# Pairing head h with head h+4 in an attention and expert kernel: fewer, larger transfers of q and k, and a new written order

## The chip, the core and the metric

The kernel runs on one core of one Trainium2 chip. The metric is device time in microseconds (us) of one execution of the whole program. The kernel before took 605.56 us as the median of three runs (602.78 to 605.9).

The core has five engines that run side by side and each in its own order: TensorE (PE, matrix products), VectorE (DVE), ScalarE (ACT), GpSimd (POOL) and SyncE (SP), which here only issues transfers. Transfers are carried out by 16 DMA engines. PE writes to PSUM, a small memory of banks, and the other tiles lie in SBUF, which has 128 partitions.

## The reference

The inputs q, k, v are 8 batches x 8 heads x 576 positions x 64 values in float32. Two attentions are added: one over means of four neighbouring positions (144 of them), repeated four times, and one in which a position sees only those less than four away. The result, as 4608 rows of 512 values (8 heads side by side), goes through a feed-forward part with 1024 hidden values.

```python
q_d, k_d, v_d = (t.reshape(B, H, 144, 4, D).mean(axis=3) for t in (q, k, v))
out_up = np.repeat(sm_attn(q_d, k_d, v_d), 4, axis=2)
mask = np.abs(pos[:, None] - pos[None, :]) < 4
out_local = softmax(where(mask, q @ k.T / 8, -1e9)) @ v
x = (out_up + out_local).transpose(0, 2, 1, 3).reshape(4608, 512)
h = x @ w_in
solu = h * softmax(h)
out = (solu - mean) / sqrt(var + 1e-6) * g_ln @ w_out
```

w_in and w_out come in as float64, 8 bytes a value.

## The kernel before

**Tiles.** The eight heads of a batch are held as four pairs. A tile such as `qT` has 128 partitions, 64 of them for each head of a pair, and four pairs along its rows. Pair r holds heads 2r and 2r+1. The rows of a 128-row block of w_in then belong to one pair, because the feed-forward part multiplies a tile `xh` of 128 tokens pair by pair with `wi_h[:, cc]`.

**Loading q and k.** For batches 0 and 1 (`EarlyBatch`), `load_one` (L477 to L483) brings one pair of q or of k in one transfer of 288 KB, and PE transposes it (L496). For batches 2 to 7 `load_q_k` (L244) brings them in a layout that VectorE can transpose in blocks of 32 x 32: 128 partitions are four quadrants of 32, one for each head of the pair and each half of its 64 values. One call brings one pair with 8 transfers of 72 KB (four quadrants, q and k), so a batch has 32 transfers, each of 32 x 18 pieces of 128 bytes. `pair_steps` then transposes k (L423), sums it by fours (`kd`), transposes q (L427) and sums it. There is one buffer for q and one for k.

**Values.** `load_vw` (L256) brings windows of 64 positions for the local attention, `load_vs` and `load_tail` (L277, L284) bring v for the sums by fours. `Local` and `PairOfLocals` compute the local attention of one and of two groups of windows, `Pooled` the other.

**Weights.** `Weights` (L300) has 16 pieces of 512 KB: eight of w_in (block cc of 128 rows, half n of the columns) and eight of w_out. `load(n)` brings one with one transfer (L325); `piece(n)` makes float32 of it and splits it into a high and a low part, with seven steps on ScalarE, VectorE and GpSimd (L334 to L374). The pieces of w_in with numbers 0, 1, 6 and 7 pass through the tile `stage`, the others through tiles named `w`.

**The feed-forward part.** 36 tiles of 128 tokens. `ffn_in` has 24 matmuls into `h` (L779), which need all eight pieces of w_in, then the softmax steps; the tile `e` is stored to `u` in DRAM (L827) and read back rearranged as `v` (L859), transposed on VectorE (L880), split into `uh` and `ul` (L886, L889), and multiplied with w_out in 24 matmuls into `o` (L903). `osb` is the scaled result (L910), stored at L912.

**Order.** The Python loops at the end only make a list of steps, `plan`, batch by batch. The work is emitted in the order of the numbers in `ORDER`, an order over all steps written out by hand or by a search; every engine executes its instructions in that order, and SP its transfers. `OTHER` is the list of steps that use the other of two engines for a step that either can do (`engine(usual, instead)`): for instance `ul` goes to VectorE and not to GpSimd. `keep_clock` steps are matmuls on a tile of zeros, 24 in all, placed in the first 110 us.

Of the kernel before, what the change touches and what calls it, by code (L numbers as in the profile page):

```python
# [124 lines left out]
def pooled_local_attention_then_solu_ffn(  # L125
# [10 lines left out]
    nc = tc.nc  # L136
    P = 128
    B, H, S, D = q.shape
    FAC = 4
# [245 lines left out]
    class Batch:  # L385
# [27 lines left out]
        def load_q_k(self, pr):  # L413
            load_q_k(self.qk, self.b, pr)
# [650 lines left out]
```

## Time and profile before

| what | value |
|---|---|
| median of three runs | 605.56 us |
| the profiled execution's own time | 605.33 us |
| its span, first to last instruction | 603.5 us |
| mean granted TensorE clock | 0.963 of full speed |
| busy: PE, VectorE, ScalarE, GpSimd | 93, 76, 51, 51% of the span |
| moved by DMA | 99.70 MB in 208,271 packets, mean 165 GB/s |

The page of the profile has the busy time of each engine, the span in 40 slices with tenths of busy time, and the chain of work that ended last. A line such as "L249" is a line of the kernel. "SPq" is the queue of SyncE: time in which a transfer was being issued. "PEld" is the loading of weights into TensorE, which overlaps with its products. "PEclk" and "granted clock" are the share of full clock that TensorE was given. The DMA share is the mean busy share of the 16 DMA engines. A packet is one contiguous piece that one DMA engine moves.

### The profile page before, as it was taken

To read this page: it belongs to the slowest core of one execution; us is meant where nothing else is said; L and a number is where in the kernel's file an instruction comes from. 1 tells how busy PE (TensorE), PEld (TensorE's weight loads), DVE (VectorE), ACT (ScalarE), POOL (GpSimd) and SP (SyncE) were. 2 spreads that over 40 slices of the span, in tenths; PEclk is the share of its full clock that TensorE was granted. 3 is DMA by queue.
4 is the path that set the end of the run, shared out by engine and by line. 5 is a ranking of instruction groups with operands and counts; after the bars stand their busy time and mean duration, and the time that the engine had idled before them with its cause. 6 is when DMAs were issued, how large, how long until landed. Compare 5 with 4: busy or idle time off the path is not lost.

```text
span 603.5 us, 16899 instructions
## 1 busy us (share of the span) xinstructions
PE 560.4 (93%) x6728; PEld 436.9 (72%) x6728; DVE 459.0 (76%) x716; ACT 306.1 (51%) x639; POOL 308.1 (51%) x457
## 2 busy tenths in 40 slices
PE   7877978799899999979989999998999999999996
PEld 4655656577677777757767777776877777787885
DVE  3999987999787888768877876777888867654641
ACT  2466763576544564544534654454534547342443
POOL 5476574657385374554635564544637523532111
PEclk9698998799899999989998999998999999999999
DMA  8998658876878677797587877667672642333230
GB/s 237 243 233 147 136 123 171 210 185 136 189 182 161 194 205 206 136 250 185 153 216 155 207 206 168 160 164 183 182 196 77 200 136 81 107 122 123 88 123 35
DMA packets 208271, 99.70 MB, mean 165 GB/s; under 512 B 164288, under 2 KB 194496, under 8 KB 208192
## 3 DMA queue, kind: packets, MB, share of 16 engines
q1 hardware_dynamic: 208192, 98.62, 65.1%
q8 instruction: 53, 0.87, 0.6%
q14 instruction: 26, 0.21, 0.1%
HBM read 65.54 MB, written 27.79 MB: 155 GB/s over the span
## 4 chain that ended last, share of the span: by engine, by line
PE 42%; DVE 16%; SPq 16%; DMA 12%; issue 6%; POOL 5%; ACT 2%; DVEq 0%; POOLq 0%; ACTq 0%
PE h L779 18%; PE o L903 18%; SPq L249 6%; SPq L666 4%; DMA w<-in_moe_w_out_dram 2%; DMA stage<-in_moe_w_in_dram 2%; SPq L859 2%; PE po L755 2%; DMA v<-u 2%; SPq L268 2%; DMA qm<-in_q_dram 1%; DVE nmx L787 1%; DMA u<-e 1%; DVE kd L381 1%; PE sd L717 1%
## 5 line engine op out<-in xcount | busy, mean ns | idle before, releaser
L903 PE MATMUL o<-wo_h,uh 128*128 128x512 f32 x288 | 118.1, 410 | 5.4 <-ACT osb L910 5.4
L779 PE MATMUL h<-wi_h,xh 128*128 128x512 f32 x288 | 119.7, 416 | 1.4 <-DVE e L794 1.4
L779 PE MATMUL h<-wi_l,xh 128*128 128x512 f32 x288 | 116.6, 405 | 0.0
L779 PE MATMUL h<-wi_h,xl 128*128 128x512 f32 x288 | 116.3, 404 | 0.0
L903 PE MATMUL o<-wo_l,uh 128*128 128x512 f32 x288 | 115.0, 399 | 0.0
L889 POOL TENSOR_TENSOR ul<-v,uh 128x512 fp32r<-128x512 f32 x46 | 60.8, 1325 | 53.2 <-ACT uh L886 41.9
L903 PE MATMUL o<-wo_h,ul 128*128 128x512 f32 x288 | 79.5, 398 | 0.0
L791 ACT ACTIVATE e<-h,nmx 128x1024 f32<-128x1024 f32 x36 | 40.1, 1115 | 68.4 <-DVE nmx L787 64.2
L903 PEld LDWEIGHTS o<-wo_h,uh 128*128 128x128 f32 x288 | 54.7, 190 | 21.0 <-ACT osb L910 6.2
L779 PEld LDWEIGHTS h<-wi_h,xh 128*128 128x128 f32 x288 | 56.0, 194 | 16.7 <-DVE e L794 2.0
L880 DVE STREAM_TRANSPOSE v<-v 128x512 f32<-128x512 f32 x70 | 46.5, 690 | 25.6 <-DMA v<-u 24.5
L779 PEld LDWEIGHTS h<-wi_h,xl 128*128 128x128 f32 x288 | 55.9, 194 | 14.0 <-DVE xl L937 0.3
L779 PEld LDWEIGHTS h<-wi_l,xh 128*128 128x128 f32 x288 | 56.0, 194 | 12.4
L903 PEld LDWEIGHTS o<-wo_h,ul 128*128 128x128 f32 x288 | 54.7, 190 | 13.3
L886 ACT ACTIVATE uh<-v 128x512 fp32r<-128x512 f32 x70 | 42.9, 623 | 41.0 <-DVE v L880 21.9
L903 PEld LDWEIGHTS o<-wo_l,uh 128*128 128x128 f32 x288 | 54.8, 190 | 11.9
L787 DVE TENSOR_REDUCE nmx<-h 128x1 f32<-128x1024 f32 x36 | 43.6, 1211 | 24.5 <-PE h L779 24.5
L794 DVE SCALAR_TENSOR_TENSOR e<-h,e 128x1024 f32<-128x1024 f32 x36 | 43.6, 1212 | 14.4 <-ACT e L791 14.4
L799 POOL TENSOR_SCALAR nmu<-su 128x1 f32<-128x1 f32 x36 | 8.5, 237 | 76.9 <-DVE e L794 75.7
L836 ACT ACTIVATE e<-e 128x1024 f32<-128x1024 f32 x35 | 36.8, 1052 | 20.5 <-DMA u<-e 20.5
L817 ACT ACTIVATE e<-e,nmu 128x1024 f32<-128x1024 f32 x24 | 27.6, 1148 | 32.2 <-POOL nmu L799 32.2
L910 ACT ACTIVATE osb<-o,s 128x512 f32<-128x512 f32 x36 | 24.5, 679 | 32.3 <-PE o L903 13.5
(122 smaller groups left out, 1042.7 us busy)
## 6 DMA issues: line engine op xcount, KB each, us to landing
u<-e SPq DMA_DIRECT2D x35, 512.0 KB, 3.3
v<-u SPq DMA_DIRECT2D x140, 128.0 KB, 3.4
out_dram<-osb SPq DMA_DIRECT2D x36, 256.0 KB, 2.9
vs<-in_v_dram SPq DMA_DIRECT2D x64, 128.0 KB, 3.6
qm<-in_q_dram SPq DMA_DIRECT2D x96, 72.0 KB, 2.9
km<-in_k_dram SPq DMA_DIRECT2D x96, 72.0 KB, 2.5
vw<-in_v_dram SPq DMA_DIRECT2D x80, 64.0 KB, 2.9
vw<-in_v_dram SPq DMA_DIRECT2D x40, 128.0 KB, 3.3
```

The lines of the kernel that those rows point to most:

```text
L249: nc.sync.dma_start(t[nm][Q * 32:Q * 32 + 32, pr], src[b, 2 * pr + par, :, dh * 32:dh * 32 + 32].rearrange("(k t) d -> t k d", t=32),)
L779: nc.tensor.matmul(hps[:, n, :], src[:, cc, :], wt[:, cc, n * 512:(n + 1) * 512], start=(cc == 0 and src is xh and wt is wi_h), stop=(cc = ...
L787: nc.vector.tensor_reduce(out=nmx, in_=hf, op=ALU.max, axis=AX.X, negate=True)
L791: nc.scalar.activation(e, hf, AF.Exp, bias=nmx, scale=1.0, accum_out=se)
L794: nc.vector.scalar_tensor_tensor(out=e, in0=hf, scalar=1.0, in1=e, op0=ALU.mult, op1=ALU.mult, accum_out=su)
L817: nc.scalar.activation(e, e, AF.Identity, bias=nmu, scale=1.0)
L836: nc.scalar.activation(e0, e, AF.Square, accum_out=m2)
L880: nc.vector.transpose(vg, vg)
L886: nc.scalar.activation(uh, tp, AF.Copy)
L889: (usual if v is None else engine(usual, nc.vector)).tensor_tensor(out=ul, in0=tp, in1=uh.bitcast(F32), op=ALU.subtract)
L903: nc.tensor.matmul(o, src[:, j, :], wt[:, 4 * g + j, :], start=(g == 0 and j == 0 and src is uh and wt is wo_h), stop=(g == 1 and j == 3 a ...
L910: nc.scalar.activation(osb, o, AF.Copy, scale=s)
```

## The change

Pair r now holds heads r and r+4. The four heads of one parity of all pairs (heads 0 to 3, or 4 to 7) are then neighbours in DRAM, and one transfer with one stride brings one quadrant of q, or of k, for all four pairs: 288 KB, 32 x 72 pieces of 128 bytes. `load_q_k` is called eight times a batch with one transfer each (first the four quadrants of k in the list, then those of q), and not four times with eight each; the list of steps is 24 longer (1871). The transposes and sums of the four pairs stay as they were.

The other places that name heads follow: v's windows, v for the sums, the tail and the early batches' q and k are read with the new head numbers, in as many transfers of the same sizes as before. The blocks of w_in now take the 64 rows of head r and the 64 rows of head r+4, in one transfer as before.

`ORDER` is a new order of all steps; it was found by a search in which transfers came late at random. `OTHER` is new too, 77 steps and not 78: among others `ul` is on VectorE 21 times and not 12, the sum of `vs` 6 times and not 3, the subtraction in `PairOfLocals` 2 times and not 5.

```diff
-    def load_q_k(t, b, pr):
-        for nm, src in (("q", q), ("k", k)):
-            for par in range(2):
-                for dh in range(2):
-                    Q = 2 * par + dh
-                    nc.sync.dma_start(
-                        t[nm][Q * 32:Q * 32 + 32, pr],
-                        src[b, 2 * pr + par, :, dh * 32:dh * 32 + 32].rearrange(
-                            "(k t) d -> t k d", t=32
-                        ),
-                    )
+    def load_q_k(t, b, nm, Q):
+        src = {"q": q, "k": k}[nm]
+        par, dh = divmod(Q, 2)
+        nc.sync.dma_start(
+            t[nm][Q * 32:Q * 32 + 32],
+            src[b, 4 * par:4 * par + 4, :, dh * 32:dh * 32 + 32].rearrange(
+                "r (k t) d -> t r k d", t=32
+            ),
+        )
...
-                    v[b, par::2, s0:s0 + W, :].rearrange("h s d -> s h d"),
+                    v[b, 4 * par:4 * par + 4, s0:s0 + W, :].rearrange("h s d -> s h d"),
...
-            src = v[b, 2 * w + par, 0:(NKB - 1) * KB * FAC].rearrange(
+            src = v[b, 4 * par + w, 0:(NKB - 1) * KB * FAC].rearrange(
...
-            src = v[b, 2 * w:2 * w + 2, (NKB - 1) * KB * FAC:].rearrange(
+            src = v[b, w::4, (NKB - 1) * KB * FAC:].rearrange(
...
+            by_pair = w_in.rearrange("(a r d) c two -> r a d c two", a=2, d=D)
             self.src = [
-                w_in[cc * P:(cc + 1) * P, n * 512:(n + 1) * 512, :]
-                for cc in range(NCC) for n in range(2)
+                by_pair[cc, :, :, n * 512:(n + 1) * 512, :] for cc in range(NCC) for n in range(2)
             ] + [w_out[fc * P:(fc + 1) * P, :, :] for fc in range(NFC)]
...
-                t, src[self.b, 2 * pr:2 * pr + 2].rearrange("h (p t) d -> p h (t d)", t=self.TT)
+                t, src[self.b, pr::4].rearrange("h (p t) d -> p h (t d)", t=self.TT)
...
-                            bt.vw[u + n][rows(wi), 2 * pr + par, :],
+                            bt.vw[u + n][rows(wi), 4 * par + pr, :],
...
-            else:
-                step(bt.load_q_k, pr)
+            elif pr == 0:
+                for nm in ("k", "q"):
+                    for Q in range(4):
+                        step(bt.load_q_k, nm, Q)
```

The numbers in `ORDER` and `OTHER` are left out here.

More of the change, by code (lines that the diff above doesn't have):

```diff
@@ L411, in room, with load_q_k @@
             }
-        def load_q_k(self, pr):
-            load_q_k(self.qk, self.b, pr)
+        def load_q_k(self, nm, Q):
+            load_q_k(self.qk, self.b, nm, Q)
         def load_v(self, u):
```

181 rows, old and new, of tables (ORDER, OTHER) are left out of this document.

## The prediction

> **What bounds the kernel now.** I read the page first: busy line, slices, chain of waits.
>
> ```profile
> span 603.5 us, 16899 instructions
> PE 560.4 (93%) x6728; PEld 436.9 (72%) x6728; DVE 459.0 (76%) x716; ACT 306.1 (51%) x639; POOL 308.1 (51%) x457
> ...
> PE   7877978799899999979989999998999999999996
> ...
> PEclk9698998799899999989998999998999999999999
> ...
> PE 42%; DVE 16%; SPq 16%; DMA 12%; issue 6%; POOL 5%; ACT 2%; DVEq 0%; POOLq 0%; ACTq 0%
> ```
>
> TensorE is the bound: 560.4 of 603.5 us. An order can only win from the 43.1 us that it idles and from slow clock after gaps. Next, the windows by stage (span; PE, PEld, DVE, ACT, POOL busy; granted clock; DMA share; GB/s).
>
> ```profile
> 0.00:45.00 45.00, 34.43 (x550) 24.95 (x551) 34.83 (x60) 20.48 (x50) 25.81 (x30) 0.89 0.94 238
> 45.00:130.00 85.00, 70.67 (x1184) 52.20 (x1180) 75.64 (x124) 50.11 (x102) 51.44 (x53) 0.90 0.74 159
> 130.00:300.00 170.00, 161.18 (x2096) 127.18 (x2095) 139.47 (x220) 91.25 (x193) 98.81 (x150) 0.98 0.76 183
> 300.00:450.00 150.00, 145.88 (x1664) 114.53 (x1662) 115.91 (x174) 74.04 (x156) 76.73 (x117) 0.97 0.73 181
> 450.00:590.00 140.00, 139.86 (x1207) 111.81 (x1207) 91.70 (x139) 65.60 (x134) 53.65 (x104) 1.00 0.37 119
> ```
>
> PE idles 10.6, 14.3, 8.8, 4.1 and 0.1 us in these stages: it is lost early. The first 45 us are the stage of the transfers (share 0.94), the next 85 that of VectorE (75.6 of 85). The first h matmul needs all eight pieces of w_in; it starts here (timeline), behind the last step of such a piece on VectorE:
>
> ```profile
> 57.62 0.69 DVE L349 SCALAR_TENSOR_TENSOR w<-stage,w 128x512 int32<-128x512 int32 x1
> ...
> 65.29 0.50 PE L779 MATMUL h<-wi_h,xh 128*128 128x512 f32 x1
> ```
>
> **The part that I expect to decide: w_in's rows.** `Weights.src` took 128 consecutive rows of w_in for piece (cc, n). It now takes two blocks of 64 rows, 256 rows apart (`a=2, d=64`). They can't be joined into one run of rows, so the source is a pattern of 2 x 64 x 4 KB where it was 128 x 4 KB. What does that do to the spread over the 16 DMA engines? Here is one 512 KB transfer by itself (transfers in the window 540.9 to 543.6) and the loads of w_in (by source line):
>
> ```profile
> DMA packets 145, 0.54 MB, mean 200 GB/s; under 512 B 16, under 2 KB 16, under 8 KB 144
> ...
> q1 hardware_dynamic: 144, 0.52, 47.7%
> ...
> u<-e SPq DMA_DIRECT2D x1, 512.0 KB, 2.6
> ```
> ```profile
> L325 SPq DMA_DIRECT2D stage<-in_moe_w_in_dram x4: 346/386/1068, 0.7 to 38.3; - x4
> L325 SPq DMA_DIRECT2D w<-in_moe_w_in_dram x4: 346/398/499, 2.6 to 19.6; - x4
> ```
>
> The lone transfer has 128 packets of 4 KB and 16 small ones, one completion for each engine. Its time is 47.7% of 2.7 us on 16 engines: 20.6 us of engine time, 0.161 us a packet. Spread over 16 engines a w_in piece costs each 1.3 us; if it is divided by its outermost count, two engines do 64 packets each, 10.3 us, and the eight pieces hold those two for 82.4 us. Every other transfer is also dealt to these two engines, in turn, and waits behind.
>
> Which end? Every transfer of this trace has an outermost count of 128, 96, 64, 32 or 16, all multiples of 16, so the rows neither confirm nor exclude a division by that count. 1.3 and 10.3 us are both open, and the nearest row (the lone transfer) gives the price of either, not the choice. As w_in's new pattern is the one that leaves this family, I take two engines, at two chances in three. The Trainium skill ("DMA: Bandwidth & Descriptors", section "Why a DMA increments its semaphore by 16 and not by 1") says that the division is by the slowest dimension other than 1, over the largest count up to 16 that divides it on both sides; by that rule it is two engines here and the sum below stands, without it the sum of the rival. No run here shows a spread below 16 yet.
>
> When does the last piece land then? In the new ORDER these stand ahead of `weights.load(7)` on SP's queue: the other seven pieces, 14 q or k loads of batches 0 and 1 (288 KB), three vw loads (four of 64 KB each), two vs (four of 128 KB) and the tail (four of 32 KB): 6.1 MB beside w_in. At the first window's rate (238 GB/s at share 0.94, so 253 when full) that is 24 us of each engine; at the lone transfer's (4096 B in 0.161 us, 407 GB/s over 16) 15 us. Landing: 0.7 + 82.4 + 15 to 24 = 98 to 107 us. Behind it come Abs and clamp, and then VectorE's 16 instructions between that piece's shift and `ffn_in(0)` in the new ORDER, about 11 us by these rows (grouped by form), among them four like the first two and three like the third:
>
> ```profile
> L345 DVE SCALAR_TENSOR_TENSOR w<-w,w 128x512 int32<-128x512 int32 x12 | 10.5, 878 | 0.2
> L349 DVE SCALAR_TENSOR_TENSOR w<-w,w 128x512 int32<-128x512 int32 x12 | 10.0, 840 | 0.1
> L551 DVE TENSOR_TENSOR pl<-sc,mask 128x512 f32<-128x512 f32 x20 | 13.4, 676 | 0.8 <-PE sc L539 0.7
> L336 DVE TENSOR_SCALAR w<-w 128x512 f32<-128x512 f32 x12 | 6.5, 538 | 4.8 <-ACT w L334 4.7
> L334 ACT ACTIVATE w<-w 128x512 f32<-128x512 f32 x12 | 8.0, 670 | 15.1 <-DMA w<-in_moe_w_out_dram 10.8 <-DMA w<-in_moe_w_in_dram 2.3 <-POOL wo_l L374 2.0
> ```
>
> Before, the way from the last such step to h was 65.3 - 56.9 = 8.4 us, so I use 8.4 to 12 (0.67 + 0.54 + 11). The first h starts between 98 + 8.4 = 106 and 107 + 12 = 119 us, which is 41 to 54 us later than 65.3; middle 48. Nothing covers it: PE executes in order, and ahead of `ffn_in(0)` stand only the matmuls of batch 0 and the first of batch 1, about as many as before. Behind it the same list of matmuls follows.
>
> **The q and k loads.** 192 transfers of 576 packets become 48 of 2304; packets and bytes stay. By source line (ns min/median/max), by timeline and by the transfers of 180 to 188.4:
>
> ```profile
> L249 SPq DMA_DIRECT2D qm<-in_q_dram x96: 311/496/1697, 49.5 to 413.5; - x96
> L249 SPq DMA_DIRECT2D km<-in_k_dram x96: 312/496/2015, 55.9 to 417.2; - x96
> ...
> DMA to landing us min/median/max: 2.0/2.6/5.5
> ```
> ```profile
> L262 SPq DMA_DIRECT2D vw<-in_v_dram x40: 595/634/2392, 197.1 to 472.8; - x40
> ```
> ```profile
> L268 SPq DMA_DIRECT2D vw<-in_v_dram x80: 595/615/1921, 30.8 to 456.1; - x80
> ```
> ```profile
> 184.06 2.12 SPq L249 DMA_DIRECT2D qm<-in_q_dram  x4
> ```
> ```profile
> 180.00:188.40 8.40, 7.26 (x106) 5.79 (x106) 6.93 (x11) 4.89 (x8) 6.55 (x9) 1.00 0.84 140
> ```
>
> An issue costs SP 0.496 us, 95 us for 192. For a transfer of four times the packets there is no row. From below: L262 has 512 packets and L268 256, and they differ by 19 ns, so 1728 more packets add 0.13 us: 0.63 x 48 = 30 us, 65 saved. From above: SP is held while the packets drain, four times 0.53 us each, 102 us, nothing saved. I take the lower price, its rows being the direct comparison. But the DMA engines are at 0.84 while four loads go out per 2.12 us, so delivery can quicken only to 0.84 of it: a batch's 32 loads from 17.0 to 14.3 us.
>
> What is SP's time worth? The chain shows one place where it ends in an idle PE:
>
> ```profile
> 254.02 1.75 SPq L249
> ...
> 256.95 3.13 DMA u<-e
> ...
> 262.46 7.41 PE o L903 x24
> ...
> 331.64 5.60 PE h L779 x24
> ```
> ```profile
> PE o L903 <- ACT osb L910: 5.4, 2, 4.1
> ```
>
> The u store waits behind 24 loads, PE waits 4.1 us for osb, and the next 24 matmuls take 7.41 instead of 5.60: 5.9 us at most. Against it: a transpose of any pair now needs all four quadrants (1.18 MB, 1.18 / (140 / 0.84) = 7.1 us from the first packet) where it needed its own four loads (2.1 us), and a quadrant can be loaded only when all four pairs of the batch before are transposed. In the new ORDER batch 3's last three k loads and batch 6's last two stand at the same place among the matmuls as the first k transposes: up to 5 us late at two places, hidden if SP has run ahead to them. I take -4 for loads and order together, from -12 (a quarter of the idle) to +12 (both waits, each with 1 us of slow clock).
>
> **OTHER, vs, tails, early loads.** ul goes from VectorE 12 times to 21:
>
> ```profile
> L889 POOL TENSOR_TENSOR ul<-v,uh 128x512 fp32r<-128x512 f32 x46 | 60.8, 1325 | 53.2 <-ACT uh L886 41.9 <-issue 4.5 <-DMA qm<-in_q_dram 3.8
> ...
> L889 DVE TENSOR_TENSOR ul<-v,uh 128x512 fp32r<-128x512 f32 x24 | 18.7, 778 | 10.2 <-ACT uh L886 10.1
> ```
>
> That is 7 us more on VectorE and 12 less on GpSimd; other moves go both ways (`pl` subtracts leave VectorE, `vs` sums come). After 450 us VectorE has 48 us to spare. Zero, inside the range above; without that cover at most 7 us. The heads' strides change in vs, tail, vw and the early loads, not their counts: zero.
>
> **Sum**, against the profiled execution's own time of 605.33 us (span 603.5, 1.8 around it; the median of the runs is 605.56): 605.3 + 48 - 4 = 649. Own range 605.3 + 41 - 12 = 634 to 605.3 + 54 + 12 = 671.
>
> **Rivals.**
> *All 16 engines serve w_in; the loads win.* No +48. SP's 16% of the chain speaks for it, PE's 0.1 us of idle after 450 against a large gain. Place: 130 to 450 us, where 12.9 us idle; price: 5.9 us at the store, and as much again of that idle as SP's 65 us reach, so about -7: 598 (592 to 602). It holds from the point that a piece lands before 45 us, as now. Faster, where I forecast slower.
> *All 16 engines, late quadrants.* Two waits of 5 us with slow clock and no gain: 605.3 + 10 = 615, with some gain 609. For it the equal places in ORDER, against it that SP issues ahead.
> *It does not do what it says.* SP is held for the packets, the engines stay at 0.84, PE's order is as full as before: 605.
>
> **How the numbers follow.** Chances: two engines 0.67, loads win 0.22, late quadrants 0.06, nothing 0.05. A measurement here tells from no change about 0.5%, 3 us. So faster 0.22, same 0.05, slower 0.73. The range from 596 to 668 holds most of the first case (0.6), the two between (0.11) and a fair part of the second (0.13). The likeliest case alone is 634 to 671.
>
> **What would show it.** Right: the w_in loads land 10 us apart or more, DMA share in the first 90 us is low (two of 16 engines: near 0.13 plus the rest's), the last `w<-stage` step is near 105 us and the first h near 112, and from there to the end the time is within 10 us of the 538 us before. Wrong: the first h before 70 us with the share again at 0.9. Of the loads: 0.63 us an issue and under 35 us in all, or about 2 us each. Late quadrants would be waits of kT for km with idle PE at sc of batches 3 and 6. The u store should go out without 24 loads ahead of it.

## The result and the profile after

The changed kernel takes 653.68 us (median of four runs, 649.22 to 655.75); the kernel before 605.53 (602.78 to 605.9). The ratio is 1.0796, with a 95% interval from 1.0725 to 1.0866. The forecast was 649.

The page of the changed kernel, in the same parts as before:

```profile
span 650.1 us, 16688 instructions
PE 559.6 (86%) x6728; PEld 435.3 (67%) x6728; DVE 461.2 (71%) x724; ACT 309.8 (48%) x645; POOL 293.7 (45%) x443
...
PE   3135434998999999799998999999999999999997
...
PEclk9996757698999999999998999999999999999999
DMA  2333344978799688668874867795745345422420
```

The work of TensorE is the same (559.6 us, before 560.4). The loss lies in the first seven slices, where PE is at 1 to 5 tenths and the DMA engines at 2 to 4, where they were at 6 to 9. Both idle at once. The line of the queue says why; it is quoted for the kernel before and then for the changed one (packets, MB, share of 16 engines):

```profile
q1 hardware_dynamic: 208192, 98.62, 65.1%
```
```profile
q1 hardware_dynamic: 205776, 98.61, 58.7%
```

2416 packets fewer. The loads of q and k are 144 transfers fewer, each with 16 completions: 2304. What is left is 112, which is 14 for each of the eight loads of w_in: each has two completions where it had sixteen. I read this as two engines for the transfer of 2 x 64 rows; the runs with sixteen, four and eight engines below test it.

The chain of waits of the changed kernel around the last piece of w_in, and the start of h in the timeline (start, length, what):

```profile
96.05 14.71 DMA stage<-in_moe_w_in_dram
...
110.84 0.66 ACT w L333
...
115.27 2.12 PE qp L495 x24
117.39 1.06 PE xp L589 x32
118.44 2.12 PE kp L495 x24
```
```profile
126.28 0.50 PE L778 MATMUL h<-wi_h,xh 128*128 128x512 f32 x1
```

The last piece is issued at 96.05 and in use at 110.84; h starts at 126.3 and not at 65.3. In between the chain runs over PE at a low clock: 24 transposes take 2.12 us (367 ns each in the median, 246 in e1_split below). Ahead of the first h PE idles 69.8 us (126.3 less 56.5 busy), and 14.1 in the kernel before. Most of it is spent at the first transposes of q, whose loads stand among the pieces of w_in on SP's queue (us in total, times, longest; the kernel before has 2.0 there):

```profile
PE qp L495 <- DMA qm<-in_q_dram: 50.5, 4, 18.6
```

The windows of the changed kernel (columns as in the prediction), the last three shifted by the 46 us:

```profile
45.00:90.00 45.00, 17.77 (x306) 11.35 (x306) 17.05 (x30) 10.02 (x33) 11.67 (x10) 0.69 0.34 101
90.00:126.00 36.00, 24.05 (x531) 20.03 (x535) 22.04 (x37) 17.12 (x30) 14.21 (x13) 0.67 0.64 160
...
176.00:346.00 170.00, 160.76 (x2095) 125.57 (x2093) 142.34 (x221) 92.16 (x205) 100.73 (x150) 0.99 0.80 187
346.00:496.00 150.00, 148.62 (x1746) 116.84 (x1744) 124.35 (x190) 77.95 (x162) 75.00 (x115) 0.99 0.67 169
496.00:636.00 140.00, 139.69 (x1214) 110.74 (x1205) 92.87 (x140) 67.62 (x138) 46.72 (x96) 1.00 0.41 129
```

From the first h to the end the changed kernel needs 650.1 - 126.3 = 523.8 us and the kernel before 603.5 - 65.3 = 538.2. So the start loses 61.0 us and the rest wins 14.4. In that rest PE is busy 503.2 us and idles 20.6, where it was busy 509.2 and idle 29.0: of the 14.4 us, 8.4 are less idle time and 6.0 are less busy time for nearly the same matmuls (5732 and 5725), at a granted clock of 0.99 and not 0.97. Two questions for the chip: is it w_in's two engines that lose the 61, and what wins the 14?

### The profile page after: what moved, and what is told of

Its sections match the earlier page's. It is cut to its first block, busy times and chain, and to the rows that moved or that the text cites. A ratio compares the mean times of both kernels' runs of the same rounds, so it can differ in the third digit from the quotient of the medians.

```text
span 650.1 us, 16688 instructions
## 1 busy us (share of the span) xinstructions
PE 559.6 (86%) x6728; PEld 435.3 (67%) x6728; DVE 461.2 (71%) x724; ACT 309.8 (48%) x645; POOL 293.7 (45%) x443
## 4 chain that ended last, share of the span: by engine, by line
PE 48%; DMA 18%; SPq 15%; DVE 10%; issue 3%; ACT 3%; POOL 2%; DVEq 0%; POOLq 0%; ACTq 0%
PE h L778 20%; PE o L902 20%; DMA w<-in_moe_w_in_dram 3%; SPq L480 3%; SPq L267 3%; DMA v<-u 3%; DMA stage<-in_moe_w_in_dram 2%; SPq L665 2%; DMA vs<-in_v_dram 2%; DMA u<-e 2%; DMA km<-in_k_dram 2%; SPq L858 2%; SPq L324 2%; PE po L754 2%; PE xp L589 1%
## 5 line engine op out<-in xcount | busy, mean ns | idle before, releaser
L778 PE MATMUL h<-wi_h,xh 128*128 128x512 f32 x288 | 118.1, 410 | 5.0 <-DVE e L793 5.0
L778 PE MATMUL h<-wi_h,xl 128*128 128x512 f32 x288 | 114.4, 397 | 0.0
L778 PE MATMUL h<-wi_l,xh 128*128 128x512 f32 x288 | 114.4, 397 | 0.0
L778 PEld LDWEIGHTS h<-wi_h,xh 128*128 128x128 f32 x288 | 54.6, 190 | 20.3 <-issue 5.9
L888 POOL TENSOR_TENSOR ul<-v,uh 128x512 fp32r<-128x512 f32 x37 | 49.1, 1332 | 37.3 <-ACT uh L885 18.7
L778 PEld LDWEIGHTS h<-wi_h,xl 128*128 128x128 f32 x288 | 54.4, 189 | 13.2
L495 PE MATMUL qp<-ident,qm 96*64 96x96 f32 x192 | 14.7, 328 | 50.7 <-DMA qm<-in_q_dram 50.5
L786 DVE TENSOR_REDUCE nmx<-h 128x1 f32<-128x1024 f32 x36 | 43.7, 1213 | 19.5 <-PE h L778 19.4
L335 DVE TENSOR_SCALAR w<-w 128x512 f32<-128x512 f32 x15 | 6.5, 440 | 62.6 <-ACT w L333 62.6
L495 PEld LDWEIGHTS qp<-ident,qm 96*64 96x64 f32 x192 | 13.0, 197 | 53.4 <-DMA qm<-in_q_dram 35.7
```

The costliest lines, as they stand in the source:

```text
L495: nc.tensor.matmul(tp[rows(par), t // HT, at:at + self.TP], self.qk[nm, pr][:, par, t], ident[0:self.TP, 0:self.TP], start=True, stop=True,)
L778: nc.tensor.matmul(hps[:, n, :], src[:, cc, :], wt[:, cc, n * 512:(n + 1) * 512], start=(cc == 0 and src is xh and wt is wi_h), stop=(cc = ...
L786: nc.vector.tensor_reduce(out=nmx, in_=hf, op=ALU.max, axis=AX.X, negate=True)
L888: (usual if v is None else engine(usual, nc.vector)).tensor_tensor(out=ul, in0=tp, in1=uh.bitcast(F32), op=ALU.subtract)
```

## The experiments

Theory: a transfer is divided over the engines by its outermost count, and this alone makes the changed kernel slow. Rival: the new order, or quadrants that come late, make the start slow.

**Two loads of 64 rows for a piece of w_in (e1_split).**

```diff
-            nc.sync.dma_start(hl, self.src[n])
+            if n < 2 * NCC:
+                for half in range(2):
+                    nc.sync.dma_start(hl[half * D:half * D + D], self.src[n][half])
+            else:
+                nc.sync.dma_start(hl, self.src[n])
```

> The changed kernel, but each piece of w_in comes in two transfers of 64 consecutive rows. Theory (each transfer is divided by its outermost count, so the one transfer of 2 x 64 rows ran on two engines): both halves run on 16 engines, 8 x 14 more completion packets than the changed kernel and 8 x 16 for the added transfers, the first h at 60 to 70 us and not 126.3. From the first h to the end the changed kernel took 523.8 us and the kernel before 538.2; if that gain belongs to the new order and loads, 65 + 524 + 1.8 = 591 us; if it was only lent by the long wait ahead of it, 598 to 605 us. Rival (the new order or the late quadrants made the start slow): the first h stays after 100 us and the time above 640 us.

Measured: 592.18 us, ratio to the kernel before 0.9824 (0.9796 to 0.9851). It is faster than both kernels. The queue has 206016 packets: 8 x 30 more than the changed kernel, 16 completions for each of 16 halves. First h and windows:

```profile
66.04 0.50 PE L782 MATMUL h<-wi_h,xh 128*128 128x512 f32 x1
```
```profile
0.00:45.00 45.00, 29.63 (x544) 21.68 (x546) 35.72 (x63) 21.40 (x51) 20.43 (x29) 0.89 0.99 217
45.00:130.00 85.00, 74.77 (x1318) 55.92 (x1314) 74.31 (x127) 54.38 (x108) 59.16 (x63) 0.90 0.84 197
130.00:300.00 170.00, 162.13 (x2055) 127.05 (x2054) 141.50 (x217) 90.33 (x195) 98.78 (x148) 0.98 0.77 184
300.00:450.00 150.00, 148.40 (x1788) 116.34 (x1786) 124.04 (x190) 77.85 (x160) 73.77 (x112) 0.99 0.66 167
```

The loss is gone with this one edit, so the rival falls. And the 14 us were hardly lent by the long wait: from the first h to the end this kernel takes 592.0 - 66.0 = 526.0 us, the changed one 523.8. The 2.2 us between them are less than the spread of the changed kernel's four runs (6.5 us), so 12 to 14 belong to order and loads together. Against the kernel before, PE is busy 4.8 us less in the first 45 us, 4.1 more between 45 and 130, 1.0 more up to 300 and 2.5 more up to 450.

**The kernel before, w_in read as 2 x 64 rows (e2_before_two).**

```diff
-                w_in[cc * P:(cc + 1) * P, n * 512:(n + 1) * 512, :]
-                for cc in range(NCC) for n in range(2)
+                by_pair[cc, :, :, n * 512:(n + 1) * 512, :] for cc in range(NCC) for n in range(2)
```

> The kernel before with one line changed: a piece of w_in is read as 2 x 64 rows in one transfer, as in the change (its rows are then those of other heads, so its result isn't the reference's; nothing is left out). Theory of two engines: completions fall by 8 x 14 = 112 packets, the last piece lands after 95 us, the first h starts at 105 to 130 us, the time is 645 to 665 us with the old order and the old 192 loads. Rival (order or loads): 603 to 608 us as before.

Measured: 659.91 us (one run), 208080 packets, which is exactly 112 fewer. The first h starts at 122.4 us, 57 us late. The old order with the old loads loses nearly as much; the pattern of w_in is enough by itself.

**Four and eight blocks (e3_four, e4_eight).**

```diff
-            by_pair = w_in.rearrange("(a r d) c two -> r a d c two", a=2, d=D)
+            by_pair = w_in.rearrange("(a r d) c two -> r a d c two", a=4, d=D // 2)   # e4: a=8, d=D // 4
```

> The changed kernel, but a piece of w_in is read as 4 x 32 rows in one transfer (4 blocks 128 rows apart; the rows then don't fit the heads, so the result isn't the reference's; nothing is left out). Theory (division by the outermost count): 4 completions a transfer, 205776 + 8 x 2 = 205792 packets on the queue; 32 packets of 0.161 us on each of four engines, 5.2 us a piece, 41 us for eight, so the last piece lands some 41 us earlier than in the changed kernel (110.8), near 70 us; the first h at 78 to 88 us and the time 604 to 614 us. Rival (any source that isn't one run of rows is slow): as the changed kernel, 650 us.

> The same with 8 x 16 rows (8 blocks 64 rows apart; result not the reference's, nothing left out). Theory of the outermost count: 8 completions a transfer, 205776 + 8 x 6 = 205824 packets, 2.6 us a piece, 21 us for eight, which hides beside the other transfers of the first 45 us: first h at 64 to 70 us, 590 to 597 us, like e1_split with 8 issues fewer. Rival: 650 us.

Measured (one run each): 619.96 us with 205792 packets, and 605.34 us with 205824. The completions are those of 4 and 8 engines to the packet, as the theory says. The Trainium skill ("DMA: Bandwidth & Descriptors", "Why a DMA increments its semaphore by 16 and not by 1") has the number of engines by the slowest count other than 1 of both sides, and one completion for each engine that takes part; the counts of 2, 4, 8 and 16 here agree with both. The times were later than expected. These are the first h, SP's issue of the last of w_in and the DMA share (from the traces) beside the time that eight pieces hold a loaded engine, 82.4 us by the lone transfer divided out:

```
engines for w_in              16     8      4      2
eight pieces hold an engine   10.3   20.6   41.2   82.4 us
last of w_in issued by SP     45.6   52.6   67.1   96.0 us
DMA share of the first 45 us  0.99   0.77   0.50   0.30
first matmul of h             66.0   75.1   94.6   126.3 us
time of the kernel            592.2  605.3  620.0  653.7 us
```

The steps of the first h (9.0, 19.5, 31.7) follow the steps of the load (10.3, 20.6, 41.2), the last one least. I had expected eight engines to hide; they don't. A reason that fits the table: in e1_split the DMA engines are at 0.99 in the first 45 us, so there is no spare time for an uneven load, and with eight, four and two engines the others stand idle while SP issues the rest later.

**What do the merged loads win? (e5_cut, e6_old_order)** e5_cut cuts each quadrant's load into four again, in the new order:

```diff
+        for pr in range(NPR):
+            nc.sync.dma_start(t[nm][Q * 32:Q * 32 + 32, pr],
+                src[b, 4 * par + pr, :, dh * 32:dh * 32 + 32].rearrange("(k t) d -> t k d", t=32))
```

> e1_split, but each quadrant's load is cut again into four transfers of one pair each, 72 KB, issued one after the other at the same place: 192 and not 48 issues, same bytes, same packets of data, same order. Theory (the DMA engines, not SP's issuing, set how fast the loads come): e1_split + 0 to 3 us, although SP is busy some 65 us longer. Rival (the fewer issues are what is gained): e1_split + 7 us or more.

Measured: 609.63 us, ratio 1.0103 (1.0071 to 1.0135), 17 us more than e1_split, measured beside it. My theory, that issuing hardly counts, falls. The first h differs by 1.3 us only. The timelines of SP's queue, e1_split and then e5_cut, show where it goes on:

```profile
63.73 0.60 SPq L248 DMA_DIRECT2D km<-in_k_dram  x1
...
88.06 0.43 SPq L328 DMA_DIRECT2D w<-in_moe_w_out_dram  x1
...
94.68 1.96 SPq L862 DMA_DIRECT2D v<-u  x4
```
```profile
63.88 2.22 SPq L249 DMA_DIRECT2D km<-in_k_dram  x4
...
91.51 0.43 SPq L329 DMA_DIRECT2D w<-in_moe_w_out_dram  x1
...
99.71 1.97 SPq L863 DMA_DIRECT2D v<-u  x4
```

Both reach the first k load at 63.8. e5_cut issues the piece of w_out 3.5 us later and the read-back of u 5.0 us later. PE waits for that piece of w_out by way of ScalarE, which has it in its order just ahead of the step plT that PE needs. ScalarE starts on the piece at 92.8 us in e1_split, after 7.8 us of idle, and at 98.2 in e5_cut, after 11.1. The row of e1_split:

```profile
92.78 0.66 ACT L337 ACTIVATE w<-w 128x512 f32<-128x512 f32 x1 [7.83 <-DMA w<-in_moe_w_out_dram]
```

PE's own wait at plt, e1_split and then e5_cut:

```profile
PE plt L583 <- ACT plT L234: 6.1, 1, 6.1
```
```profile
PE plt L584 <- ACT plT L234: 10.3, 1, 10.3
```

SP's queue is issuing nearly all the time: summed over its timeline from 60 to 300 us, 231.5 of 240 us in the kernel before, 220.4 in e1_split, 227.9 in e5_cut. (A row of several transfers counts the short gaps within it; the issues alone are 209.6, 208.0 and 213.6.) Time in which SP is held on an issue counts in this too, so a full queue doesn't show by itself that it sets the time.

e6_old_order is e1_split with the old ORDER and OTHER; a batch's eight merged transfers are issued where its first load stood:

```diff
+        def load_once(self):
+            if not self.loaded:
+                self.loaded = True
+                for nm in ("k", "q"):
+                    for Q in range(4):
+                        load_q_k(self.qk, self.b, nm, Q)
```

> e1_split with the ORDER and OTHER of the kernel before: the pairing h, h+4 and the merged transfers stay, all eight of a batch are issued at the place where the old order has the batch's first load. Theory (the order brings what there is to bring, the loads little): 600 to 608 us, near the kernel before. Rival (the merged loads bring it): as e1_split within 3 us. A third way: all eight transfers in one place hold up others behind them on SP and DMA: above 608 us.

Measured: 617.17 us, ratio 1.0228 (1.0187 to 1.0268): the third way. Its PE waits and its window from 300 to 450 us, where PE is busy 12.5 us less than in e1_split:

```profile
PE po L762 <- POOL vd L461: 10.2, 2, 8.6
PE h L786 <- DVE e L801: 9.2, 4, 4.8
```
```profile
300.00:450.00 150.00, 135.93 (x1563) 107.01 (x1562) 109.11 (x165) 70.90 (x150) 73.87 (x113) 0.94 0.67 166
```

Why vd comes late on GpSimd there wasn't followed further. So neither half wins alone: the old order with 192 loads takes 603.0 us, the new one with 192 takes 609.6, the old one with 48 in one place 617.2, the new one with 48 592.2. How the old order would do with the 48 spread out wasn't tried, since a pair's transpose stands there ahead of loads of other pairs.

**Is it SP's issuing? (e7_issues, e13_one)** Tiny extra transfers, three or one behind each merged load:

```diff
+        for _ in range(3):   # e13_one: range(1)
+            n = extra[0]
+            extra[0] += 1
+            nc.sync.dma_start(idle[0:32, 2 * n:2 * n + 2], src[b, 4 * par, 0:32, 0:2])
```

> e1_split with three tiny extra transfers (32 pieces of 8 bytes, to a place that nobody reads) behind each of the 48 loads of a quadrant: 144 issues more, as many as in e5_cut, almost no bytes. Theory (SP's issue time is what e5_cut lost: SP is busy 39 of 40 us from 60 to 100 us): 603 to 612 us, near e5_cut's 609.6. Rival (cutting costs in the DMA engines, by smaller transfers of data): 592 to 596 us.

> e7_issues with one tiny transfer behind each quadrant's load and not three: 48 issues more than e1_split (592.2 us), where 144 more gave 650.4. Theory (SP's queue is full from 60 to 300 us, 92% there in e1_split, so each added issue at these places costs its time): a third of the 58 us, 605 to 615 us. Rival (there is room for the first ones, and it is only beyond some number that they cost): 592 to 600 us.

Measured: 650.36 us (ratio 1.0794, 1.0747 to 1.084) and 608.48 us (ratio 1.0072, 1.0043 to 1.0101). e7_issues costs far more than its theory asked, e13_one what it asked. Against e1_split's 592.2 that is 58 us for 144 issues and 16 for 48, 0.40 and 0.34 us an issue (59 and 15 when each is taken against the kernel before measured beside it). Nobody waits for these transfers, and they carry 37 KB in all. The time of the DMA engines didn't grow: their share of the span is 60.2% of 644.9 us in e7_issues and 66.3% of 592.0 in e1_split, 388 and 392 us. The issue itself, by source line (ns min/median/max), e7_issues:

```profile
L260 SPq DMA_DIRECT2D idle<-in_k_dram x72: 414/422/2307, 61.2 to 434.1; - x72
```

The read-back of u, which moves 128 KB at a time, in e1_split:

```profile
L862 SPq DMA_DIRECT2D v<-u x140: 303/430/3013, 94.7 to 567.5; - x140
```

These medians say 0.42 us, however little an issue moves. They mislead. In e13_one every tiny transfer stands directly behind a merged load, and there the same 256 bytes take 1.7 to 1.9 us in the median, while the merged loads' own rows fall to 0.43:

```profile
L260 SPq DMA_DIRECT2D idle<-in_k_dram x24: 1187/1720/2554, 59.6 to 393.9; - x24
L260 SPq DMA_DIRECT2D idle<-in_q_dram x24: 1257/1902/5079, 61.9 to 412.8; - x24
```
```profile
59.60 1.81 SPq L260 DMA_DIRECT2D idle<-in_k_dram  x1
61.46 0.42 SPq L251 DMA_DIRECT2D qm<-in_q_dram  x1
61.92 1.38 SPq L260 DMA_DIRECT2D idle<-in_q_dram  x1
```

In e7_issues the first of each three takes 1.92 us in the mean, the two others 0.47. In e1_split whatever stands directly behind a merged load (2304 packets) takes 1.9 us in the mean of 48, and behind every other kind of transfer that occurs more than once 0.4 to 0.7; that includes the stores of u, which are 512 KB but 128 packets. In the kernel before the issue behind a 72 KB load (576 packets) takes 0.60. So behind a merged load an issue's row shows that load's price and not its own. What holds SP there isn't shown; it goes with the packets ahead and not with the bytes.

e5_cut's 144 added issues cost less, 17 us, because they take the place of longer ones: all of SP's issuing sums to 390.8 us in e1_split, 413.1 in e5_cut and 457.7 in e7_issues, with spans of 592.0, 606.9 and 644.9. From this I formed a rule, 0.8 us for each us of SP's issuing, and tested it from the other side. (e13_one, which ran last, has 27.3 us more of issuing than e1_split and a span 14.5 us longer, 0.5 for each.)

**Taking issues away (e9_act, e10_out_act, e11_out_u_act, e12_no_tail).** e9_act lets ScalarE issue the 48 loads, e10_out_act the 36 stores of osb, e11_out_u_act also the 35 stores of u; e12_no_tail leaves out 28 tail loads.

```diff
-        nc.sync.dma_start(                                        # e9: t[nm][Q * 32:Q * 32 + 32]
+        nc.scalar.dma_start(
-        nc.sync.dma_start(out[i * P:(i + 1) * P, :], osb)         # e10, e11
+        nc.scalar.dma_start(out[i * P:(i + 1) * P, :], osb)
-            nc.sync.dma_start(away[i], e)                         # e11
+            nc.scalar.dma_start(away[i], e)
-                load_tail(self.vs[n], self.b)                     # e12
+                if self.b == 0:
+                    load_tail(self.vs[n], self.b)
```

> e1_split with the 48 quadrant loads issued by ScalarE instead of SyncE, at the same places of the order. Theory (SP is the serial limit from 60 to 140 us, of which these loads still take a quarter): SP reaches the w_out pieces and the u stores some 5 us earlier there, PE's 6.1 us wait at plt shrinks, 585 to 591 us. Rival (SP is no limit any more once the loads are merged, and ScalarE now issues late behind its own waits): 592 to 602 us.

> e1_split with the 36 stores of osb issued by ScalarE, which made osb itself, instead of SyncE (28.1 us of issuing there, and SyncE no longer waits for osb). Theory (SP's queue is the limit: issuing sums of 391, 413 and 458 us went with spans of 592.0, 606.9 and 644.9, 0.8 us of time for each us): 25 us less issuing in the part up to 450 us counts partly: 578 to 588 us. Rival (e7_issues and e5_cut lost by something else than SP's time, for instance the number of transfers under way): 590 to 594 us.

> e10_out_act, and the 35 stores of u issued by ScalarE too (19.2 us of issuing, and SyncE's waits for e, 47.7 us in all, mostly in the last third). Theory (SP): 4 to 10 us under e10_out_act. Rival (ScalarE's own queue pays: as in e9_act, where loads issued by ScalarE came late): above e1_split's 592.

> e1_split without the tail loads of batches 1 to 7 (28 transfers of 32 KB, 18.6 us of issuing, 0.9 of 98.6 MB; the sums then use old values, so the result isn't the reference's). Theory (SP's issuing time, 0.8 us for each): 577 to 586 us. Rival (bytes and DMA time are what counts): 590 to 593 us.

Measured: e9_act 624.84 us, ratio 1.0385 (1.0337 to 1.0433); e10_out_act 596.43, ratio 0.9859 (0.9819 to 0.9898); e11_out_u_act 613.36, ratio 1.016 (1.0119 to 1.0202); e12_no_tail 590.0, ratio 0.9771 (0.9729 to 0.9813). The rule doesn't hold in this direction. e10_out_act takes 9.7 us off SP's sum (381.1) and wins nothing, e11_out_u_act takes 35.7 off and loses 21 us; both put issues on ScalarE instead. e12_no_tail, which only leaves issues out, tests it weakly: SP's sum fell by 7.6 us and not by the 18.6 of the issues left out, since others were held longer. For 7.6 the rule gives 6 us, and 2 were won (4 when each is taken against the kernel before measured beside it), where I had asked for 15. e9_act is worse than both theory and rival; its loads come late, as the rival said, and these waited for them:

```profile
L248 ACTq DMA_DIRECT2D km<-in_k_dram x24: 318/1118/3547, 72.3 to 410.7; - x24
...
DVE qT L430: 16.6, 4
DVE kT L426: 15.0, 3
```

That SP's time is short in e1_split is shown in one direction only. A reason that fits, argued and not shown: of e1_split's span from 45 to 300 us PE idles only 18.1 us (85 - 74.77 and 170 - 162.13), so little is left to win, while every issue more moves later work past the point where PE has nothing else. It isn't excluded either that what the added issues cost comes from the number of transfers under way, and not from SP's time. Which engine limits e1_split there stays open. So does why e11_out_u_act loses 21 us against e1_split: its u stores are issued in 0.33 us each, and its PE waits are spread.

## Why the prediction was right

**What bounds.** PE's work stayed at 560 us and the time went into its idle, early, as read.

**w_in's rows.** Right, and shown from both sides: e1_split takes it away, e2_before_two adds it alone, the completions give the number of engines. The trace of before had no row for the choice between two engines and sixteen; this was the open step, taken at two in three.

**The size of it.** The first h was put at 106 to 119 us, the middle 48 us late, and started at 126.3, 61 us late. Two terms were small. The landing was put at 98 to 107 and was 110.8: the last piece was issued only at 96.05. SP itself had stood on single issues early, as in this row of the changed kernel's timeline, and didn't issue ahead; its last issue of w_in moves with the number of engines (45.6, 52.6, 67.1, 96.0 us). That the filled queues of the two engines hold it fits this, but no run takes that hold by itself:

```profile
12.18 9.55 SPq L480 DMA_DIRECT2D qm<-in_q_dram  x1
```

The way from landing to h was put at 8.4 to 12 us from VectorE's instructions and took 15.4. The chain goes over PE, whose matmuls for batch 1 stood in line behind the same wait, and the granted clock was 0.67 from 90 to 126 us. I had counted one engine's instructions on a way that changed engines.

**The loads and the order.** -4, from -12 to +12; from the first h on it was -14.4 in the changed kernel, outside that range and outside the 10 us that the prediction allowed on this stretch. e1_split, which is what the rival "the loads win" described at 598 (592 to 602), runs at 592.2, 10.8 us under the kernel before measured beside it. The price of an issue only looks right: 0.63 us for four times the packets, with medians of 0.52 and 0.50 in e1_split:

```profile
L248 SPq DMA_DIRECT2D km<-in_k_dram x24: 371/519/2648, 63.7 to 375.0; - x24
L248 SPq DMA_DIRECT2D qm<-in_q_dram x24: 383/502/2261, 64.4 to 397.7; - x24
```

By these rows all issues of q and k fell from 120.3 to 48.0 us. But the time moved into the issues behind them: those of vw grew from 83.8 to 94.3 us, of plT from 49.2 to 58.2, of osb's stores from 18.6 to 28.1. All of SP's issuing fell from 409.4 to 390.8 us, and is 22.3 less than in e5_cut, not the 65 of the prediction. The step that failed is the comparison of two loads of 256 and 512 packets by their own rows; a merged load that stands behind another kind of transfer takes 0.51 us and the issue behind it 1.9, so the end that was set aside (SP held for the packets, 102 us in all) was the nearer one. The other step, "what is SP's time worth", 5.9 us at most, was too small: I read it from the one place where the chain passed from SP into an idle PE, and in e5_cut 22.3 us of issuing went with 17 us of time. The first step was too large, the second too small, and they partly cancel inside the -4; that is luck. The prediction also named slow clock as something to win, but priced it at one place only (1.8 of the 5.9 us); 6.0 of the 14.4 us came that way.

**Late quadrants.** Didn't come: in e1_split VectorE waits 2.3 us in all for q.

**The sum.** 61.0 - 14.4 = 46.6 us was measured, 48 - 4 = 44 forecast. Both terms were too small, by 13 and by 10, and of opposite sign; that 649 lies so near 653.7 is in part luck. The cause and the direction were earned, and most of the delay at the first h.

## What to carry to other kernels

When the layout of a weight changes, look at the outermost count of its load: a source of two blocks in one transfer ran on two of the 16 engines, and two transfers of 64 rows brought back 61 us for eight issues. Before saying what merged loads save on an issuing queue, sum all of its issues and not the rows of these loads, because the time can stand in the row behind. Where the queue was over nine tenths full here, an added issue cost 0.3 to 0.4 us of the kernel's time; taking issues away gave 2 to 4 us at most. A merged transfer and the order around it are one change: here each without the other was slower than the kernel before.

## What the runs showed that I had not expected

- Spread over eight engines rather than sixteen, w_in still costs 13 us (one run), 9.0 of them at the first h.
- SP stood for up to 9.55 us on a single issue while most DMA engines were idle. The window of the changed kernel's first 45 us, where e1_split has a DMA share of 0.99:

```profile
0.00:45.00 45.00, 14.36 (x152) 10.70 (x152) 13.85 (x26) 7.59 (x11) 6.39 (x16) 1.00 0.30 95
```

- A transfer of 256 bytes takes SP 0.42 us behind another of its kind and 1.7 to 1.9 us behind a load of 2304 packets. A load's price stands in the row of whatever is issued next.
- PE's busy time shrinks with its idle time. From the first h on it is 503.2, 503.8, 509.2, 509.3 and 509.5 us for nearly the same matmuls in the changed kernel, e1_split, the kernel before, e5_cut and e6_old_order, with 20.6, 22.2, 29.0, 30.3 and 35.6 us of idle and granted clocks of 0.99, 0.98, 0.97, 0.97 and 0.96.
- Issuing from ScalarE is no free second queue: 48 loads moved there cost 33 us (624.8 against 592.2).
